# Recurrence with a block inverse, fused with an MLP: transposed input of the inverse laid out the other way round, one 16x16 merge moved from TensorE to VectorE, new instruction order

## The chip, the cores and the metric

The kernel runs on one core of a Trainium2 chip. The metric is the device time of one execution in microseconds (us); lower is better. A core has five engines that run side by side, each through its own instructions in a fixed order: TensorE (PE in the rows; PEld are its weight loads), VectorE (DVE), ScalarE (ACT), GpSimd (POOL) and SyncE (SP), which issues most of the transfers.

## What is computed

A recurrence over 768 steps for 4 x 8 heads with a 40 x 40 state each, and behind it a gated MLP on 3072 tokens. The reference, cut to its core:

```python
for t in range(S):                                   # S = 768, per batch and head
    y[:, :, t] = einsum('bhd,bhde->bhe', rt, state)
    Sa = einsum('bhde,bhe->bhd', state, at)
    state = state * wt - einsum('bhd,bhe->bhde', Sa, bt) + einsum('bhd,bhe->bhde', vt, kt)
x = y.transpose(0, 2, 1, 3).reshape(B * S, H * D)    # 3072 x 320
a, b = x @ w1, x @ w2                                # 320 x 1024 each
out = (a * b @ w3) @ w_out                           # 1024 x 1024, 1024 x 320
```

The weights come as 64-bit floats and are converted on the chip.

## The kernel before

The 768 steps are cut into 12 chunks of 64 (`NCH`, `C`). Inside a chunk the recurrence becomes matrix products and the inverse of a unit triangular 64 x 64 matrix for each head. The matrices of all heads lie in one tile: 128 partitions by 16 heads (`NPC`) by two halves of 32 columns, `JP`.

**Solve** (L648) inverts the 32 x 32 diagonal blocks, all on VectorE, as a sequence of small steps `so.x`. `f0` (tag `so.in`, L656) transposes the blocks from `JP` into the tile `TDX`. `dots` (L677) adds two steps to the sequence: a multiplication with broadcast operands into `tmp` (L680) and a sum over its last axis (L684). First the 8 x 8 triangles are inverted (seven pairs of steps with `A8` as an operand, results in `DG`), then pairs of 8 are merged to 16 x 16 (`Tp`, seen as `T32`), then pairs of 16 to 32 x 32. `A()` is the transposed input seen as row s, column t; `P8` is a piece of `TDX` that the inverse does not need, used for intermediate products. `f6` (`so.td`, L730) and `f7` (`so.tt`, L733) transpose the result back into the two halves of `TDX`.

The last merge, 16 to 32, runs in one of two ways. For chunks c >= `MERGED` it is eleven more steps on VectorE: five pairs of `dots` and one addition (L725). For chunks below `MERGED` TensorE does it after `so.tt`: 64 small products `so.m1` (L754), a copy to `Q16` on ScalarE (`so.q`), the products `so.m2`, a copy back into `TDX` (`so.t`), and a second `so.tt`.

**Join** (L766) joins the two 32 x 32 inverses of a head with the block below them: two products on TensorE (`jo.mm1`, `jo.mm2`, L782) with copies on ScalarE. `jo.mm1` needs `so.tt`; the copies `jo.tt` fill the tile `TT`, which the recurrence reads. `TDX` exists once, `JP` and `TT` twice.

**The rest.** `rec` (L870, tags `r.*`) runs the chunk's recurrence on TensorE, with ScalarE copies and VectorE masks (`r.u`, L921). `gather` moves the result into token order by transfers, `mlp` splits it into a high and a low part (`m.xh` at L971, `m.xl` at L974) and runs the MLP on TensorE: `m.mm1` (L987, eight matmuls of 256 columns a group) and `m.mm2` (L1012). `m.gl` (L1003) makes the low part of the gated product, on VectorE or GpSimd. At the start `convert` and `weights` turn the weights into matmul form (`cv.*`, `w.hi`, `w.lo` at L527), and `product` (L539) multiplies `w3` by `w_out` beforehand. The first MLP needs all of `w.lo`. The `ck.*` steps read the weights once more late in the run and check that the fast conversion was allowed; they use the tiles `JP` and `TDX` when the solves leave them free.

**Order.** Every operation is recorded first. A table of numbers written out by hand, `RANK`, gives each operation its place in the whole sequence (`place`, L300), and each engine runs its own operations in that order. A second table, `ON`, says for some kinds on which engine each instance runs (`d` VectorE, `p` GpSimd, `a` ScalarE). An instruction of GpSimd with two inputs waits for the last such instruction of VectorE placed before it ("port" in `place`).

Of the kernel before, what the change touches and what calls it, by code (L numbers as in the profile page):

```python
# [33 lines left out]
MERGED = 2  # L34
# [21 lines left out]
    "cv.sign": "aaddddaaadaaaaaaaaadaaaddaddadd",  # L56
    "cv.add": "ddddpdddddddddddddddpdpddddppdd",
    "w.lo": "dddddddddddd",
    "sc.aa": "dddddpdppddppddppdpppdpd",
    "sc.xs": "ddpdddpdddddpdpdddpdpddd",  # L60
    "m.gl": "dddpdpdpppppdpddpppppppppppppppdpppdpppdpppppddp",
    "ck.sq": "ddaaadaddaadaddddadaddddddddddd",
}
RANK = {kind: [int(n) for n in ranks.split()] for kind, ranks in {
# [1198 lines left out]
```

## Time and profile before

| | before |
|---|---|
| median of 3 runs | 624.01 us (620.47 to 626.31) |
| profiled execution: time / span | 625.69 us / 624.0 us |
| TensorE busy | 554.2 us, 89% of the span |
| VectorE busy | 514.1 us, 82% |
| ScalarE busy | 408.6 us, 65% |
| GpSimd busy | 160.4 us, 26% |
| mean granted TensorE clock | 0.971 of full speed |

The profile comes from one execution. Busy times are unions over the span; TensorE's matmuls overlap, so their mean durations are longer than the time each adds. A wait names the instruction that waits and what ended the wait. The clock is a share of full speed (2.4 GHz); the lower level is 0.5 (1.2 GHz).

### The profile page before, as it was taken

The page shows a single profiled execution, that of the slowest core. Times are in us where ns is not written, and L with a number is a line of the kernel's source. Part 1 is how long each engine was busy: PE and PEld are TensorE (multiplying, and loading weights), DVE is VectorE, ACT ScalarE, POOL GpSimd, SP SyncE. Part 2 cuts the span into 40 slices and gives each one's busy share as a digit, 9 for nine tenths or more (in the row PEclk, how much of TensorE's full clock was granted, in tenths as well). Part 3 has the DMA queues.
Part 4 walks back from the last instruction along what each step waited for, and adds up shares of the span by engine and source line. Part 5 has one row for each costly group of instructions (what it writes and reads, how often), then busy time and mean ns, then how long its engine had stood idle before and what let it go on. Part 6 is the DMA issues. An engine that isn't in the chain of part 4 may idle for free.

```text
span 624.0 us, 27212 instructions
## 1 busy us (share of the span) xinstructions
PE 554.2 (89%) x11970; PEld 498.7 (80%) x11970; DVE 514.1 (82%) x946; ACT 408.6 (65%) x883; POOL 160.4 (26%) x224
## 2 busy tenths in 40 slices
PE   0477998899998999999998999998998999999993
PEld 0355776799888988898897888898887989989993
DVE  5897897899599698896798797896996998977773
ACT  7787867954746747638646568648377568477552
POOL 3014131202521413034133133144043132131100
PEclk9997996999899899999998999999998999999998
DMA  8999777232143155322442343712643535237671
GB/s 226 293 251 268 224 222 203 71 94 81 50 107 111 33 133 141 87 72 61 112 116 66 98 112 98 193 43 72 180 117 105 153 87 148 85 83 242 212 246 56
DMA packets 56813, 83.48 MB, mean 134 GB/s; under 512 B 30320, under 2 KB 38000, under 8 KB 56688
## 3 DMA queue, kind: packets, MB, share of 16 engines
q1 hardware_dynamic: 56300, 81.34, 46.9%
q8 instruction: 96, 1.57, 1.1%
q10 hardware_dynamic: 388, 0.33, 0.2%
q14 instruction: 29, 0.24, 0.1%
HBM read 72.99 MB, written 3.93 MB: 123 GB/s over the span
## 4 chain that ended last, share of the span: by engine, by line
DVE 39%; PE 35%; ACT 10%; DMA 7%; issue 6%; POOL 1%; SPq 0%; ACTq 0%; DVEq 0%; POOLq 0%
DVE tmp L680 12%; PE bank L987 12%; PE bank L870 10%; PE bank L539 5%; DVE TDX L684 3%; DMA raw<-in_w3t_dram 3%; PE bank L1012 3%; DVE Tp L684 3%; PE bank L628 3%; DVE ga L1000 2%; ACT JP L329 2%; ACT TT L329 2%; DVE TDX L656 2%; PE bank L782 2%; DVE fm L578 2%
## 5 line engine op out<-in xcount | busy, mean ns | idle before, releaser
L987 PE MATMUL bank<-xs,W 128*128 128x256 f32 x1536 | 211.9, 291 | 0.6 <-DVE xs L974 0.6
L987 PEld LDWEIGHTS bank<-xs,W 128*128 128x128 f32 x1536 | 192.6, 193 | 8.4 <-issue 1.2
L1003 POOL TENSOR_TENSOR gl<-ga,gh 128x512 fp32r<-128x512 f32 x35 | 45.0, 1286 | 175.2 <-DVE tmp L680 52.0
L830 POOL TENSOR_SCALAR_AFFINE_SELECT vg<-vg 64x256 f32<-64x256 f32 x96 | 42.3, 447 | 124.7 <-DVE tmp L680 41.9
L1012 PE MATMUL bank<-W3h,gh 128*128 128x320 f32 x192 | 62.7, 327 | 0.7 <-ACT gh L329 0.7
L1012 PE MATMUL bank<-W3h,gl 128*128 128x320 f32 x192 | 60.1, 313 | 2.8 <-DVE gi L596 1.7
L1012 PE MATMUL bank<-W3l,gh 128*128 128x320 f32 x192 | 59.5, 310 | 0.0
L680 DVE TENSOR_TENSOR tmp<-Tp,TDX 128x256 f32<-128x256 f32 (+2 forms) x54 | 57.8, 1071 | 1.0
L628 PE MATMUL bank<-aa,xx 40*64 40x64 f32 x1536 | 31.4, 235 | 29.9 <-DVE xx L600 19.3
L628 PEld LDWEIGHTS bank<-aa,xx 40*64 40x64 f32 x1536 | 28.3, 148 | 33.2 <-issue 21.0
L329 ACT ACTIVATE JP<-bank 32x256 f32<-32x256 f32 (+2 forms) x120 | 45.5, 379 | 11.9 <-PE bank L628 7.5
L329 ACT ACTIVATE ga<-bank 128x512 f32<-128x512 f32 x48 | 28.6, 596 | 32.8 <-PE bank L987 31.8
L870 PE MATMUL bank<-un,bk 64*64 64x104 f32 (+1 forms) x768 | 44.3, 252 | 4.7 <-DVE un L921 4.1
L870 PE MATMUL bank<-hs,TT 64*64 64x104 f32 x768 | 45.1, 255 | 2.9 <-ACT TT L329 1.4
L329 ACT ACTIVATE gh<-ga 128x512 fp32r<-128x512 f32 x48 | 30.3, 631 | 25.8 <-DVE ga L1000 24.7
L644 POOL TENSOR_SCALAR_AFFINE_SELECT lm<-lm 64x512 f32<-64x512 f32 x48 | 35.3, 740 | 45.4 <-DVE tmp L680 18.0
L870 PE MATMUL bank<-vg,bk 64*64 64x104 f32 (+1 forms) x768 | 44.2, 253 | 0.0
L1000 DVE TENSOR_TENSOR ga<-bank,ga 128x512 f32<-128x512 f32 x48 | 32.9, 685 | 13.5 <-PE bank L987 7.6
L921 DVE TENSOR_TENSOR un<-bank,mask_h 128x416 f32<-128x416 f32 x48 | 28.2, 587 | 18.9 <-PE bank L870 18.6
L870 PEld LDWEIGHTS bank<-un,bk 64*64 64x64 f32 (+1 forms) x768 | 35.4, 123 | 10.0 <-DVE un L921 7.1
L539 PE MATMUL bank<-wof,w3f 128*128 128x320 f32 x128 | 42.4, 487 | 0.0
L870 PEld LDWEIGHTS bank<-hs,TT 64*64 64x64 f32 x768 | 35.2, 133 | 6.4 <-ACT TT L329 2.4
(126 smaller groups left out, 1263.7 us busy)
## 6 DMA issues: line engine op xcount, KB each, us to landing
rv<-in_rv_dram SPq DMA_DIRECT2D x24, 588.0 KB
xx<-in_fmx_dram SPq DMA_DIRECT2D x24, 448.0 KB
raw<-in_w3t_dram SPq DMA_DIRECT2D x16, 512.0 KB
JP<-in_w3t_dram SPq DMA_DIRECT2D x11, 512.0 KB
fm<-in_fmg_dram SPq DMA_DIRECT2D x24, 227.5 KB
aa<-in_fma_dram SPq DMA_DIRECT2D x24, 224.0 KB
raw<-in_w_dram SPq DMA_DIRECT2D x10, 512.0 KB
vg<-in_vt_dram SPq DMA_DIRECT2D x48, 80.0 KB
```

The costliest lines, as they stand in the source:

```text
L329: act.activation(out_, in_, AF.Copy, scale=scale)
L539: pe.matmul(out=pt.t[:, 0:DM], lhsT=w[:, j], rhs=wof[:, j], start=(j == 0), stop=(j == NJ - 1))
L628: pe.matmul(out=bank(s)[64 * z:64 * z + 64, i, p], lhsT=X[r, p, z], rhs=aa.t[r, i, p], start=True, stop=True)
L644: op("ca.mask", lambda q=q: pool.affine_select(out=lm.t[q], in_=lm.t[q], pattern=[[0, 2 * NP], [1, C]], compare_op=ALU.is_gt, fill=0.0, ba ...
L680: dve.tensor_tensor(out=scratch(*shape), in0=x().to_broadcast([128, *shape]), in1=y().to_broadcast([128, *shape]), op=ALU.mult)
L684: dve.tensor_reduce(out=out_(), in_=scratch(*shape), axis=mybir.AxisListType.X, op=ALU.add)
L830: op("pa.mask", lambda q=q, vg=vg: pool.affine_select(out=vg.t[q, :, 0:C], in_=vg.t[q, :, 0:C], pattern=[[0, NP], [1, C]], compare_op=ALU. ...
L870: pe.matmul(out=out_(ab ^ z, p), lhsT=left(ab, ab ^ x, p), rhs=right(ab ^ x, p), start=start and p == 0, stop=True, skip_group_check=True)
L987: pe.matmul(out=pt.t[:, TOK * x:TOK * x + TOK], lhsT=WT[k][:, cs], rhs=xs.t[:, z], start=(n == 0), stop=(n == 7))
L1000: op("m.ab", lambda a=a, pt=pt: dve.tensor_tensor(out=a.t, in0=wide(pt), in1=a.t, op=ALU.mult), r=[pt], w=[a])
L1003: both("m.gl", lambda e, a=a, j=j: e.tensor_tensor(out=gl.t[:, j:j + 2], in0=a.t, in1=gh.t[:, j:j + 2], op=ALU.subtract), r=[a, (gh, j)], ...
L1012: pe.matmul(out=pt.t[:, 0:DM], lhsT=l.t[:, j, ts], rhs=W3[r][:, j], start=(j == 0 and n == 0), stop=(j == NJ - 1 and n == 2))
```

## The change

Three edits in one.

1. `f0` writes the transposed input with t innermost in `TDX`: element (s, t) lies at 32 s + t, before at 32 t + s. The views `A`, `A8` and `P8` follow: `A` now has stride 1 along t, 32 along s; `P8` moves to the last 256 words, rows 24 to 31 of the new layout. The output of the transposing instruction is no longer contiguous.
2. `MERGED` goes from 2 to 1: chunk 1's last merge runs on VectorE, as in the chunks behind it. Chunk 0 keeps TensorE.
3. `RANK` and `ON` are new throughout.

```diff
-MERGED = 2
+MERGED = 1
 ON = {
-    "w.lo": "dddddddddddd",
+    "w.lo": "ddppdpdddddp",
-    "m.gl": "dddpdpdpppppdpddpppppppppppppppdpppdpppdpppppddp",
+    "m.gl": "dddpdpddpppppppppdpppppdddpppppddppdpppdpddddddp",
 RANK = ...
         def f0():
             src = jp.t[:, :, 0].rearrange("q p t -> q t p").unsqueeze(2).to_broadcast([128, 32, 2, 16])
-            dve.transpose(out=tdx.t.rearrange("q (t r p) -> q t r p", r=2, p=16), in_=src)
+            dve.transpose(out=tdx.t.rearrange("q (r p t) -> q t r p", r=2, p=16), in_=src)
 
         def A():
-            return tdx.t.rearrange("q (t s) -> q s t", s=32)
+            return tdx.t.rearrange("q (s t) -> q s t", t=32)
 
         def A8(s):
-            v = tdx.t[:, 33 * s + 32:33 * s + 33]
-            return bass.AP(v.tensor, v.offset, (v.ap[0], (264, 4), (32, 7 - s)))
+            v = tdx.t[:, 33 * s + 1:33 * s + 2]
+            return bass.AP(v.tensor, v.offset, (v.ap[0], (264, 4), (1, 7 - s)))
 
         def P8():
-            return tdx.t[:, 0:256].rearrange("p (q s) -> p q s", s=32)[:, :, 8:24]
+            return tdx.t[:, 768:1024].rearrange("p (q s) -> p q s", s=32)[:, :, 0:16]
```

Counted over the whole table `ON`: `m.gl` runs on VectorE 13 times before and 20 after (35 and 28 on GpSimd); `w.lo` 12 and 8 (0 and 4 on GpSimd); `sc.xs`, the scaling of `xx`, 18 and 17 (6 and 7); `cv.sign` 12 and 11 (19 and 20 on ScalarE); `ck.sq` 22 and 15 (9 and 16 on ScalarE).

TensorE in chunk 1, around the join, before. `rv,SB` are the recurrence's products with the state, `TDX,Q` is `so.m2`, `wof,w3f` the weight product, `TDX,JP` at L782 the join, `un,aa` the next step of the recurrence:

```order
L870 MATMUL bank_156<-rv_122,SB 40x104 x2
L870 MATMUL bank_154<-rv_122,SB 40x104 x2
L754 MATMUL bank_153<-TDX_121,Q_83 32x16 x64
L539 MATMUL bank_155<-wof,w3f_178 128x320 x4
L782 MATMUL bank_157<-TDX_121,JP_145 32x32 x32
L539 MATMUL bank_155<-wof,w3f_178 128x320 x4
L782 MATMUL bank_153<-TDX_121,JP_145 32x32 x32
L870 MATMUL bank_158<-un_129,aa_114 64x104 x2
```

The same place after:

```order
L870 MATMUL bank_152<-un_129,aa_114 64x104 x2
L870 MATMUL bank_155<-un_130,aa_114 64x104 x2
L539 MATMUL bank_154<-wof,w3f_177 128x320 x4
L782 MATMUL bank_157<-TDX_121,JP_145 32x32 x32
L539 MATMUL bank_154<-wof,w3f_177 128x320 x4
L782 MATMUL bank_153<-TDX_121,JP_145 32x32 x32
L628 MATMUL bank_158<-aa_113,xx_109 64x64 x2
```

The products `so.m1` and `so.m2` of chunk 1 are gone, and the recurrence step with `un,aa` stands ahead of the join instead of behind it.

VectorE at the end of chunk 1's solve, before: from the first `so.tt` (L733) to the second, with steps of the weight conversion (L453, L460, L446, L544) and of the next chunk's scaling between them:

```order
L733 STREAM_TRANSPOSE TDX_121<-TDX_121 128x512
L578 SCALAR_TENSOR_TENSOR fm_106<-fm_106,first 104x520
L453 TENSOR_SCALAR rs_167<-raw_165 128x512
L544 TENSOR_TENSOR W3l<-bank_154,W3h 128x320
L592 TENSOR_TENSOR gt_120<-fm_106,gi_119 104x512
L596 SCALAR_TENSOR_TENSOR gi_119<-gt_120,gi_119 104x512
L460 ISA w3f_178<-w3f_178,rs_169 128x1024
L600 TENSOR_TENSOR xx_109<-xx_109,gi_119 104x1024
L460 ISA mf_172<-mf_172,rs_167 128x1024
L446 TENSOR_SCALAR mf_171<-raw_164 128x512
L578 SCALAR_TENSOR_TENSOR fm_105<-fm_105,first 104x520
L733 STREAM_TRANSPOSE TDX_121<-TDX_121 128x512
```

The end of the same solve after:

```order
L684 TENSOR_REDUCE Tp<-tmp 128x8x8
L930 TENSOR_TENSOR y_142<-bank_154,fm_105 104x4x64
L680 TENSOR_TENSOR tmp<-Tp,TDX_121 128x512
L684 TENSOR_REDUCE R_151<-tmp 128x8x8
L725 TENSOR_TENSOR TDX_121<-R_151,TDX_121 128x8x8
L578 SCALAR_TENSOR_TENSOR fm_106<-fm_106,first 104x520
L680 TENSOR_TENSOR tmp<-TDX_121,DG 128x512
L684 TENSOR_REDUCE Tp<-tmp 128x8x8
L730 STREAM_TRANSPOSE TDX_121<-Tp 128x32x16
L592 TENSOR_TENSOR gt_120<-fm_106,gi_119 104x512
L544 TENSOR_TENSOR W3l<-bank_153,W3h 128x320
L733 STREAM_TRANSPOSE TDX_121<-TDX_121 128x512
```

The steps of the merge stand where the wait for the second `so.tt` was filled with other work; there is one `so.tt`.

TensorE at chunk 2's join, before. `xs,W` are matmuls of the first MLPs:

```order
L987 MATMUL bank_156<-xs_1769,W_1_1481 128x256 x2
L987 MATMUL bank_156<-xs_1769,W_3_1482 128x256
L987 MATMUL bank_156<-xs_1769,W_4_1483 128x256 x2
L782 MATMUL bank_152<-TDX_121,JP_144 32x32 x32
L987 MATMUL bank_153<-xs_1769,W_0_102 128x256 x2
```

After:

```order
L987 MATMUL bank_156<-xs_1611,W_1_1327 128x256 x2
L987 MATMUL bank_156<-xs_1611,W_3_1328 128x256
L987 MATMUL bank_156<-xs_1611,W_4_1329 128x256 x2
L782 MATMUL bank_152<-TDX_121,JP_144 32x32 x32
L987 MATMUL bank_155<-xs_1611,W_0_102 128x256 x2
```

The join has not moved against the MLP groups around it.

## Rows read from the trace of the kernel before

**Rows 1.** Busy us (and instructions) of each engine by stage; stage, length first.

```profile
0.00:124.00 124.00, 87.13 (x2116) 67.17 (x2120) 101.04 (x197) 97.17 (x198) 30.98 (x56) 0.93 0.80 220
124.00:560.00 436.00, 412.68 (x9200) 380.04 (x9189) 374.18 (x667) 276.14 (x626) 121.71 (x162) 0.98 0.38 101
```

The columns are PE, PEld, DVE, ACT, POOL, then PE's clock, the DMA share and GB/s.

**Rows 2.** TensorE's waits from 124 to 560: us in total, times, longest.

```profile
PE bank L782 <- DVE TDX L733: 5.9, 6, 1.7
PE bank L870 <- DVE un L921: 3.7, 8, 0.7
...
PE bank L987 <- DVE xs L974: 0.6, 1, 0.6
```

**Rows 3.** The chain that ended last, by engine and line; L680's busy time.

```profile
DVE 39%; PE 35%; ACT 10%; DMA 7%; issue 6%; POOL 1%; SPq 0%; ACTq 0%; DVEq 0%; POOLq 0%
DVE tmp L680 12%; PE bank L987 12%; PE bank L870 10%; PE bank L539 5%; DVE TDX L684 3%; DMA raw<-in_w3t_dram 3%; PE bank L1012 3%; DVE Tp L684 3%; PE bank L628 3%; DVE ga L1000 2%; ACT JP L329 2%; ACT TT L329 2%; DVE TDX L656 2%; PE bank L782 2%; DVE fm L578 2%
...
0.00:560.00 560.00, 109.45 (x182) 0.97 0.47 128
```

**Rows 4.** VectorE by shape in solve: count | busy us, mean ns | idle before.

```profile
L680 DVE TENSOR_TENSOR tmp<-Tp,TDX 128x512 f32<-128x512 f32 x20 | 22.4, 1118 | 0.5
...
L680 DVE TENSOR_TENSOR tmp<-Tp,TDX 128x1024 f32<-128x1024 f32 x10 | 20.5, 2054 | 0.1
...
L680 DVE TENSOR_TENSOR tmp<-Tp,TDX 128x256 f32<-128x256 f32 x24 | 14.9, 623 | 0.4
...
L680 DVE TENSOR_TENSOR tmp<-TDX,DG 128x512 f32<-128x512 f32 x20 | 14.4, 720 | 0.5
L684 DVE TENSOR_REDUCE Tp<-tmp 128x64 f32<-128x512 f32 x20 | 13.7, 686 | 0.5
...
L684 DVE TENSOR_REDUCE TDX<-tmp 128x64 f32<-128x1024 f32 x10 | 12.2, 1217 | 0.2
...
L680 DVE TENSOR_TENSOR tmp<-TDX,DG 128x256 f32<-128x256 f32 x24 | 10.3, 431 | 0.3
...
L725 DVE TENSOR_TENSOR TDX<-R,TDX 128x64 f32<-128x64 f32 x10 | 2.2, 225 | 0.3
```

**Rows 5.** The same view: the transposes, and two multiplications on strided operands.

```profile
L656 DVE STREAM_TRANSPOSE TDX<-JP 128x1024 f32<-128x1024 f32 x12 | 24.1, 2011 | 4.1 <-ACT JP L329 2.7 <-PE bank L782 1.3
...
L730 DVE STREAM_TRANSPOSE TDX<-Tp 128x512 f32<-128x512 f32 x12 | 13.3, 1105 | 0.4
...
L733 DVE STREAM_TRANSPOSE TDX<-TDX 128x512 f32<-128x512 f32 x14 | 9.9, 709 | 2.8 <-ACT TDX L329 2.4
...
L696 DVE TENSOR_TENSOR tmp<-DG 128x128 f32<-128x128 f32 x12 | 4.8, 402 | 0.3
L703 DVE TENSOR_TENSOR Tp<-tmp,DG 128x128 f32<-128x128 f32 x12 | 4.7, 393 | 0.3
```

**Rows 6.** The merge on TensorE, two chunks; a piece of the chain (start, us).

```profile
L754 PE MATMUL bank<-TDX,Q 32*32 32x16 f32 x256 | 3.9, 206 | 3.9 <-issue 2.1 <-ACT Q L329 1.7
...
L754 PE MATMUL bank<-TDX,JP 32*32 32x16 f32 x256 | 2.5, 180 | 0.0
...
123.39 0.94 ACT xs L971 x2
```

**Rows 7.** Two stretches behind waits for the solve, columns as in rows 1.

```profile
156.00:164.00 8.00, 6.87 (x160) 6.68 (x161) 3.76 (x5) 5.54 (x12) 4.96 (x5) 0.79 0.36 93
336.00:344.00 8.00, 6.43 (x157) 5.95 (x156) 4.64 (x6) 6.56 (x15) 5.64 (x9) 0.79 0.27 83
```

**Rows 8.** Groups of instructions: the low part of the gated product, and `w.lo`.

```profile
L1003 POOL TENSOR_TENSOR gl<-ga,gh 128x512 fp32r<-128x512 f32 x35 | 45.0, 1286 | 175.2 <-DVE tmp L680 52.0 <-ACT gh L329 37.5 <-ACT gi L582 25.9
...
L1003 DVE TENSOR_TENSOR gl<-ga,gh 128x512 fp32r<-128x512 f32 x13 | 9.2, 711 | 1.3 <-ACT gh L329 1.3
...
L527 DVE TENSOR_TENSOR W<-mf,W 128x512 fp32r<-128x512 f32 (+1 forms) x12 | 8.5, 719 | 3.7 <-ACT W L329 3.7
```

More of the change, by code (lines that the diff above doesn't have):

```diff
@@ L55 @@
 ON = {
-    "cv.sign": "aaddddaaadaaaaaaaaadaaaddaddadd",
-    "cv.add": "ddddpdddddddddddddddpdpddddppdd",
-    "w.lo": "dddddddddddd",
-    "sc.aa": "dddddpdppddppddppdpppdpd",
-    "sc.xs": "ddpdddpdddddpdpdddpdpddd",
-    "m.gl": "dddpdpdpppppdpddpppppppppppppppdpppdpppdpppppddp",
-    "ck.sq": "ddaaadaddaadaddddadaddddddddddd",
+    "cv.sign": "dddadaaaddddaaaadaaaaaaddaaaaaa",
+    "cv.add": "dddddddddddddddddddppdpdpdpdddd",
+    "w.lo": "ddppdpdddddp",
+    "sc.aa": "ddddddddpdpppppppdppddpd",
+    "sc.xs": "ddddddpppdddddpdddpdpdpd",
+    "m.gl": "dddpdpddpppppppppdpppppdddpppppddppdpppdpddddddp",
+    "ck.sq": "dddaaddadaaaaadddadaaaddaadadda",
 }
 RANK = {kind: [int(n) for n in ranks.split()] for kind, ranks in {
[184 rows of a table removed]
[184 rows of a table added]
 }.items()}
```

366 rows, old and new, of the table RANK are left out of this document.

## The prediction

> **What bounds the kernel now.** I read first how busy the engines are by stage. Up to 124 us (weight conversion and the first two chunks) DVE works 101.04 of 124 us and TensorE 87.13; from 124 to 560 us TensorE works 412.68 of 436 us and DVE 374.18 [rows 1]. So in the long middle stage TensorE has only 436 − 412.68 = 23.3 us of idle time and DVE 61.8 us: work taken off DVE cannot shorten the stage by itself, it can only close TensorE's gaps.
>
> Then I read what ends TensorE's waits in that stage. The largest entry is L782 (the first product of `join`) waiting for L733 (the last transpose of `solve`): 5.9 us in 6 waits, the longest 1.7 [rows 2]. Four of the ten solves are finished before TensorE asks for them, six are late. The next is L870 waiting for L921 (`r.u`), 3.7 us in 8 short waits. Last I read the chain that ended last: DVE holds 39% and TensorE 35% of the span, and L680, the multiplications inside `solve`, alone 12% [rows 3]. The chain hops from DVE (solve) to TensorE (join, recurrence, MLP) and back, once in a chunk. The reader should see a kernel that two in-order engines limit in turns, with TensorE the tighter.
>
> **The solve's reads.** In `solve` the multiplications of `dots` read the transposed input `A()` with the last axis t innermost. Before, neighbours in t lie 32 words apart; after, they are adjacent. The price of a 32-word hop stands in the trace: with `A()` as an operand 512 elements take 1118 ns and 1024 take 2054, that is (2054 − 1118)/512 = 1.83 ns per element; the same instruction on contiguous operands (`tmp<-TDX,DG`) takes 431 for 256 and 720 for 512, 1.13 ns per element [rows 4]. So I price the new forms by the contiguous rows: 256 elements 623 → 431, 512 elements 1118 → 720, and 1024 elements 2054 → 720 + 2 × (720 − 431) = 1298. A solve that merges on DVE has two of 256, two of 512 and one of 1024 (24, 20 and 10 in the run): 2 × 0.192 + 2 × 0.398 + 0.756 = 1.94 us less. The seven small multiplications with `A8` keep a second operand (`DG`, 8 words apart in its inner axis); L696, which reads two strided operands, takes 402 ns for 128 elements and L703 with one takes 393 [rows 5]. One strided operand costs nearly all that two cost, so I give these seven no gain.
>
> The Trainium skill says the same of such reads (Vector Engine (DVE) Microarchitecture Reference, section 5.2, Measured stream behaviour on trn2): a port runs at full rate only on runs of at least two adjacent words, 1.054 ns per column against 1.73 with one source hopping; by its figures the 1024 form would save 0.69 us, by the rows 0.76.
>
> **The transposing input (L656)** is where the hop goes to. It reads `JP` 64 words apart already, and from now on it also writes 32 words apart. Now it takes 2011 ns for 1024 elements. No row has both. Bounds: nothing, if the read hides the write; or the whole price of a strided write, L730 (strided write, 1105 ns for 512) less L733 (contiguous, 709), 0.396 for 512, so 0.79 us here [rows 5]. The nearest pair, L696 against L703, gives 9 ns on 128, 0.07 on 1024; I take 0.1 us a solve, 1.2 over twelve, and keep 0.79 (9.5 over twelve) for the range. The transpose loses 0.1, so a full solve is 1.84 us shorter.
>
> **Chunk 1's merge.** The two products and two copies go (`so.m1`, `so.m2`, `so.q`, `so.t`), with one L733 of 0.71. L754 has 3.9 + 2.5 us in two chunks, so TensorE loses 3.2 us of work [rows 6]. DVE gains eleven instructions: multiplications 0.72, 1.30, 0.72, 0.72, 0.72, four reductions of 512 at 0.69 and one of 1024 at 1.22, one addition of 64 elements at 0.23 [rows 4]: 4.18 + 2.76 + 1.22 + 0.23 = 8.4 us. Net on DVE in chunk 1: 8.4 − 0.7 − 2 × 0.19 + 0.1 = +7.4. This lies before 124 us, where the first MLP waits for its last weights: the chain there ends in ACT's `xs` at 123.39 [rows 6], TensorE waits 0.6 us for it [rows 2]. I cost both parts at nothing: TensorE's 3.2 us is hidden by that wait, DVE's 7.4 by its 23 us of idle time before 124 us and by four `w.lo` that go from DVE to POOL (4 × 0.72 = 2.9 [rows 8]). On TensorE the join of chunk 1 now waits for a solve that is longer on DVE but needs no second trip over TensorE and ACT; queued behind it are the rest of the `W3` product and chunk 1's recurrence, which the first MLP does not need. Without that cover the first MLP starts 7.4 − 2.9 = 4.5 us later.
>
> **The order.** The places are alike: in chunk 2 the join's first product still stands between the same MLP matmul groups. No transfer is added or taken away; SP's issues change places by a few, which I cost at nothing (a late first load would show in the last rival's stretch). Of the choices of engine one bears on the middle stage: `m.gl` goes from POOL to DVE seven times net, 7 × 0.711 = 5.0 us more on DVE and 7 × 1.286 = 9.0 less on POOL [rows 8]. On DVE they stand in front of solve steps; I charge the chain's DVE share, 39%, so 2.0 us. Seven `ck.sq` go from DVE to ACT; these check pieces lie late in the run, ACT works 276.14 of the 436 us of the middle stage [rows 1], and I cost them at nothing; uncovered they would be 7 × 0.72 = 5 us on ACT (by the 512-column row of L527 [rows 8]).
>
> **The sum.** Six waits for the solve, none longer than 1.7 us, against solves shorter by 1.84: −5.9. The clock: after the two longest of them TensorE's granted clock is 0.79 on average over 8 us, a part of it at the lower level of 1.2 GHz instead of 2.4, after TensorE stood idle [rows 7]; where the engine is busy that is 2 × 8 × 0.21 = 3.4 us lost, given back when the waits go. Against that +2.0 for `m.gl`. Together −5.9 − 3.4 + 2.0 = −7.3 us. The profiled execution took 625.69 us (span 624.0), so 618.4 by its own time; it is 1.7 above the median of the runs shown, 624.01, and by that the forecast is 616.7. What is late next is `r.u`, the copies of `TT` and the last check pieces at the end; none of these does the change touch.
>
> **Rivals.**
> *DVE is the real bound.* For: it holds 39% of the chain, and L680's 12% of 624 is 75 us out of its 109.45 [rows 3]. Then 68% of what the multiplications lose in ten solves, 0.68 × 19.4 = 13.2, comes off, the dips with it: −13.2 − 3.4 + 2.0 = −14.6, 609. Against: TensorE's 23 us of gaps would have to shrink by more than half.
> *TensorE is the bound and the gaps only move.* Its waits for `r.u` and the other short ones grow as the solve's shrink, the idle and the clock dips stay; with half of the 5.9 won and the 2.0 paid, 623.
> *The transpose pays in full.* With 0.79 for the write a solve is 1.15 us shorter, so the waits of 1.7 and the next below it stay in part (about 1.0 us of the 5.9) and so do the dips: −4.9 + 2.0, 621. For: L730 shows that a strided write costs as much as a strided read. The skill's same section has a destination stepping 24 words at 2.50 ns per column, against 1.73 for a hopping source; by that the transposes would lose 12 × 0.79 = 9.5 us, the same as this bound. L730's 1105 for 512, about 1.9 per element with its fixed part, does not show the 2.50.
> *Slower: chunk 1's merge holds up the first MLP.* If DVE's idle time before 124 us lies where the merge cannot use it (it waits there for ACT and for weight data), the first MLP starts 4.5 us late or, if the `w.lo` on POOL finish late too, the whole 7.4 us late. TensorE has nothing else to do then, and everything behind shifts. It decides from 7.3 us on, when it eats all of the later gain; with the gaps staying as well it is 624 + 7.4 = 631.
>
> **How the numbers follow.** The forecast, 616.7 with an own range of 612 to 621, has 0.45; DVE as the bound 0.17; the gaps that move 0.17; the transpose in full 0.11; the late MLP 0.10. A measurement of this kernel can tell about 1% from no change, so faster means below 617.8 and slower above 630.2. Faster: seven tenths of the forecast's case and all of the first rival, 0.48; slower: nearly all of the last, 0.09; the rest 0.43. The range runs from 607 to 626: it leaves out the late MLP and the low end of the first rival.
>
> **What would show it.** In the profile after, the multiplications with `A()` at about 0.43, 0.72 and 1.30 us for 256, 512 and 1024 elements; L656 near 2.1 (2.8 would be the rival); the seven `A8` products unchanged. TensorE's wait for L733 should fall from 5.9 us to under 1.5, its idle time between the first MLP and 560 us from 23 to about 17, and the clock should stay at the upper level after chunk 2's join. The first `xs` should still start near 123 us; at 128 or later the last rival holds. I am wrong if the solve waits go and another entry of the same size stands in their place, or if the stage before the first MLP has become longer.

## The result and the profile after

The changed kernel takes 605.72 us (median of 4 runs, 601.54 to 607.49) against 625.16 us for the kernel before beside it; the ratio is 0.968, with a 95% interval of 0.959 to 0.977. The profiled execution took 607.17 us, its span 605.5. Measured again beside the layout alone, the ratio was 0.972 (0.967 to 0.976). The gain is 2.9 to 3.2%, 17 to 20 us, where 616.7 us, 1.2%, was forecast; the time lies just below the range of 607 to 626.

First the multiplications of the solve. VectorE by shape in the changed kernel (count | busy us, mean ns | idle before):

```profile
L656 DVE STREAM_TRANSPOSE TDX<-JP 128x1024 f32<-128x1024 f32 x12 | 26.7, 2226 | 6.8 <-ACT JP L329 3.8 <-ACT TT L329 3.0
...
L680 DVE TENSOR_TENSOR tmp<-Tp,TDX 128x512 f32<-128x512 f32 x22 | 15.2, 693 | 0.4
L680 DVE TENSOR_TENSOR tmp<-TDX,DG 128x512 f32<-128x512 f32 x22 | 15.2, 692 | 0.4
...
L680 DVE TENSOR_TENSOR tmp<-Tp,TDX 128x1024 f32<-128x1024 f32 x11 | 13.6, 1239 | 0.2
...
L680 DVE TENSOR_TENSOR tmp<-Tp,TDX 128x256 f32<-128x256 f32 x24 | 11.1, 461 | 0.4
...
L680 DVE TENSOR_TENSOR tmp<-DG,TDX 128x196 f32<-128x196 f32 x12 | 6.2, 516 | 0.3
```

With `A()` as an operand 512 elements now cost what the contiguous instruction costs (693 and 692 ns), 1024 take 1239 and 256 take 461; the prices were right within 0.06 us [rows 4]. The largest `A8` product barely moves, from 527 to 516 ns; the seven together take 0.17 us less in a solve. The transpose L656 takes 2226 ns, not 2011 [rows 5]: 0.22 us more for writing 32 words apart as well.

Then the stages, cut at the first and the eleventh `m.xl` (L974), which stands on VectorE at the start of an MLP. Before, then after (stage, length, then busy PE, PEld, DVE, ACT, POOL; PE's clock, DMA share, GB/s):

```profile
0.00:124.30 124.30, 87.43 (x2132) 67.47 (x2133) 101.04 (x197) 97.47 (x200) 30.98 (x56) 0.93 0.80 220
124.30:556.70 432.40, 409.08 (x9071) 376.83 (x9062) 373.22 (x666) 272.64 (x619) 119.90 (x160) 0.98 0.37 101
556.70:624.00 67.30, 57.70 (x779) 54.43 (x777) 39.86 (x83) 38.51 (x67) 9.50 (x9) 0.96 0.61 187
```

```profile
0.00:119.20 119.20, 85.48 (x1824) 64.12 (x1828) 105.10 (x204) 96.49 (x197) 28.59 (x56) 0.94 0.76 223
119.20:535.60 416.40, 401.23 (x9057) 370.54 (x9052) 351.69 (x667) 274.99 (x619) 122.52 (x159) 0.99 0.39 106
535.60:605.50 69.90, 60.06 (x866) 56.24 (x854) 37.50 (x83) 42.72 (x74) 5.22 (x8) 0.94 0.59 181
```

The first stage is 5.1 us shorter, the middle one 16.0, the last one 2.6 longer. In the middle TensorE's idle time falls from 23.3 to 15.2 us and its busy time by 7.9 us, although it runs nearly the same number of matmuls there (9071 and 9057 in the profile); the granted clock is 0.99 of full speed, not 0.98. The first stage scatters: two executions of one and the same kernel, the layout alone below, have their first `m.xl` at 122.1 and at 125.0 us, so the 5.1 us there need not all be the change's.

TensorE's waits in the middle stage after (us in total, times, longest):

```profile
PE bank L870 <- DVE un L921: 6.4, 8, 1.5
PE bank L870 <- issue: 3.9, 5, 2.1
...
PE bank L628 <- POOL aa L589: 0.4, 1, 0.4
PE bank L782 <- DVE TDX L733: 0.2, 1, 0.2
```

The 5.9 us of waiting for the solve [rows 2] are 0.2. `r.u` (L921) holds TensorE for 6.4 us where it was 3.7.

And the chain that ended last, which before was DVE 39% and PE 35% [rows 3]:

```profile
PE 47%; DVE 17%; ACT 16%; DMA 8%; issue 5%; SPq 4%; POOL 1%; ACTq 0%; DVEq 0%; POOLq 0%
```

These shares are coarse: in two executions of the layout alone DVE has 17% and 25%.

### The profile page after: what moved, and what is told of

Same layout as the page of the kernel before. It is cut to its first block, busy times and chain, and to the rows that moved or that the text cites. A ratio compares the mean times of both kernels' runs of the same rounds, so it can differ in the third digit from the quotient of the medians.

```text
span 605.5 us, 26713 instructions
## 1 busy us (share of the span) xinstructions
PE 546.8 (90%) x11714; PEld 490.9 (81%) x11714; DVE 494.3 (82%) x950; ACT 414.2 (68%) x889; POOL 156.3 (26%) x222
## 4 chain that ended last, share of the span: by engine, by line
PE 47%; DVE 17%; ACT 16%; DMA 8%; issue 5%; SPq 4%; POOL 1%; ACTq 0%; DVEq 0%; POOLq 0%
PE bank L987 19%; PE bank L870 12%; PE bank L1012 5%; ACT JP L329 4%; ACT TT L329 4%; PE bank L539 3%; SPq L946 3%; DVE tmp L680 3%; PE bank L628 2%; PE bank L845 2%; DMA raw<-in_wo_dram 2%; DMA raw<-in_w3t_dram 2%; PE bank L821 1%; DVE TDX L656 1%; DVE un L921 1%
## 5 line engine op out<-in xcount | busy, mean ns | idle before, releaser
L987 PE MATMUL bank<-xs,W 128*128 128x256 f32 x1536 | 209.0, 288 | 0.0
L987 PEld LDWEIGHTS bank<-xs,W 128*128 128x128 f32 x1536 | 190.1, 191 | 7.3 <-issue 0.8
L830 POOL TENSOR_SCALAR_AFFINE_SELECT vg<-vg 64x256 f32<-64x256 f32 x96 | 40.3, 426 | 145.9 <-DVE tmp L680 72.2
L1003 POOL TENSOR_TENSOR gl<-ga,gh 128x512 fp32r<-128x512 f32 x28 | 36.1, 1290 | 121.7 <-DVE tmp L680 46.1
L870 PE MATMUL bank<-un,bk 64*40 64x104 f32 (+1 forms) x768 | 44.8, 255 | 10.0 <-DVE un L921 7.8
L644 POOL TENSOR_SCALAR_AFFINE_SELECT lm<-lm 64x512 f32<-64x512 f32 x48 | 33.5, 699 | 76.2 <-DVE tmp L680 25.4
L329 ACT ACTIVATE JP<-bank 64x256 f32<-64x256 f32 (+2 forms) x120 | 45.2, 378 | 10.8 <-PE bank L628 8.3
L870 PE MATMUL bank<-hs,TT 64*64 64x104 f32 x768 | 46.6, 260 | 2.2 <-ACT TT L329 1.7
L870 PEld LDWEIGHTS bank<-un,bk 64*40 64x40 f32 (+1 forms) x768 | 35.7, 124 | 13.6 <-DVE un L921 11.2
L921 DVE TENSOR_TENSOR un<-bank,mask_h 128x416 f32<-128x416 f32 x48 | 28.1, 584 | 22.7 <-PE bank L870 22.6
L870 PE MATMUL bank<-vg,bk 64*40 64x104 f32 (+1 forms) x768 | 45.0, 255 | 0.3 <-issue 0.2
L870 PEld LDWEIGHTS bank<-hs,TT 64*64 64x64 f32 x768 | 36.7, 136 | 7.5 <-ACT TT L329 3.0
L680 DVE TENSOR_TENSOR tmp<-Tp,TDX 128x256 f32<-128x256 f32 (+2 forms) x57 | 39.9, 700 | 1.0
```

Of the source, the lines that this page charges most:

```text
L329: act.activation(out_, in_, AF.Copy, scale=scale)
L644: op("ca.mask", lambda q=q: pool.affine_select(out=lm.t[q], in_=lm.t[q], pattern=[[0, 2 * NP], [1, C]], compare_op=ALU.is_gt, fill=0.0, ba ...
L680: dve.tensor_tensor(out=scratch(*shape), in0=x().to_broadcast([128, *shape]), in1=y().to_broadcast([128, *shape]), op=ALU.mult)
L830: op("pa.mask", lambda q=q, vg=vg: pool.affine_select(out=vg.t[q, :, 0:C], in_=vg.t[q, :, 0:C], pattern=[[0, NP], [1, C]], compare_op=ALU. ...
L870: pe.matmul(out=out_(ab ^ z, p), lhsT=left(ab, ab ^ x, p), rhs=right(ab ^ x, p), start=start and p == 0, stop=True, skip_group_check=True)
L921: dve.tensor_tensor(out=un[i].t, in0=view(hp[i]), in1=mask_h.unsqueeze(1).to_broadcast([128, NP, N]), op=ALU.mult)
```

## The experiments

Each ratio is against the kernel before in the same session. The first four split the change.

**The layout alone.** The four edits of `f0`, `A`, `A8` and `P8`; everything else is as before:

```diff
-            dve.transpose(out=tdx.t.rearrange("q (t r p) -> q t r p", r=2, p=16), in_=src)
+            dve.transpose(out=tdx.t.rearrange("q (r p t) -> q t r p", r=2, p=16), in_=src)
...
```

> Only the layout of the transposed input is new; MERGED stays 2, order and engine choices are those of before. Both theories: a full solve is 1.94 us shorter on its multiplications and 0.2 longer on the transposing input, VectorE loses about 17 us of work. Theory SOLVE (the gain is the shorter solve on the chain between the two engines): most of the 18.5 us between the two profiled spans appears with the old order, 13 us or more, ratio below 0.980. Theory ORDER (the new order makes the gain, the solve's waits alone are worth my 7 us or less): ratio 0.988 to 0.998.

Measured: 606.82 us, 0.975 (0.971 to 0.979). The layout brings 15 us with the order of before, where my sum had 9.3 for it (5.9 for waits and 3.4 for the clock), and it brings most of what the whole change brings.

**The new order without the layout**: the changed kernel with the four edits undone.

> The changed kernel with the old layout: new order, MERGED = 1, but reads 32 words apart. VectorE gets about 19 us of work back (eleven full solves at 1.94 less 0.2 for the transpose). Theory SOLVE: the new order was made for short solves and cannot hide long ones; 620 us or more, ratio 0.99 to 1.01. Theory ORDER: 608 to 614, ratio 0.975 to 0.985.

Measured: 619.01 us, 0.994 (0.991 to 0.997). New order and `MERGED = 1` are worth 3.7 us by themselves. The ratio is the one that the theory of the solve gave, though the time lies a little below its 620: the order is no loss with long solves, and it is a small part.

**MERGED = 1 alone**, old layout and old order:

```diff
-MERGED = 2
+MERGED = 1
...
```

In the table `RANK` the eleven merge steps of chunk 1 get evenly spaced places between its two old `so.tt`, with `so.td` behind them, and one `so.tt` is left out.

> Only MERGED = 1: the eleven merge steps of chunk 1 are put evenly between the places of its two old output transposes, everything else stands as before. My prediction gave it nothing (0 to +7.4 us if the first MLP is held up). Theory that the round trip over TensorE and ACT in chunk 1 cost the early stage time: 2 to 5 us faster, ratio 0.992 to 0.997. Theory that VectorE's 8.4 us of added work hold up the first MLP: 4 to 7 us slower, ratio 1.007 to 1.012.

Measured: 626.8 us, 1.0065 (1.0033 to 1.0097): 4 us slower. In its profile the first `m.xl` stands at 127.2 us, 26.1 us after the last piece of weights is asked for (101.1); before, it is 19.7 us after it (104.7), and in the two executions of the layout alone 20.7 and 20.6. The merge on VectorE does hold up the first MLP when the order is not made for it. It costs 4 us, where 7.4 was the price without any cover (in this run all `w.lo` stay on VectorE).

**Layout and MERGED = 1 under the old order.**

> Layout and MERGED = 1 together under the old order and engine choices. Theory SOLVE: close to the changed kernel, ratio 0.970 to 0.980. Theory ORDER: like e1, ratio 0.985 to 0.998; the distance to the changed kernel's 0.968 is then the order's own share.

Measured: 609.53 us, 0.980 (0.974 to 0.986); its first `m.xl` too stands late, at 127.0, 25.0 us after the last weights are asked for. By the middles of the intervals, which overlap, the steps add up: the layout gives 15, `MERGED = 1` costs 3 to 4, the new order gives that back and a little more.

Two runs ask which solves count, the seven others keeping the old layout.

```diff
+NEW = (2, 5, 6, 7, 10)          # the second run: (3, 4, 8, 9, 11)
-            return tdx.t.rearrange("q (t s) -> q s t", s=32)
+            return tdx.t.rearrange("q (s t) -> q s t" if c in NEW else "q (t s) -> q s t", s=32)
...
```

**The five solves that TensorE visibly waits for.**

> Before, with the new layout only in chunks 2, 5, 6, 7 and 10, the five solves that TensorE visibly waits for at the join (5.5 us of the 5.9). The other seven solves keep the old layout. Theory WAITS (my prediction: only the solves that are late at the join matter): all of the layout's gain, 12 to 15 us, ratio 0.975 to 0.982. Theory CHAIN (VectorE runs through the middle stage without slack that matters, every solve's 1.7 us come off in full): half of the gain, 6 to 9 us, ratio 0.986 to 0.991.

**Five solves that are ready when TensorE asks.**

> Before, with the new layout only in chunks 3, 4, 8, 9 and 11, the solves that are ready when TensorE asks. Theory WAITS: no gain, 0 to 2 us, ratio 0.997 to 1.0. Theory CHAIN: as much as in the five others, 6 to 9 us, ratio 0.986 to 0.991.

Measured: 612.54 us, 0.980 (0.978 to 0.982), and 615.69 us, 0.986 (0.983 to 0.989). The first came out as the theory of the waits had it, the second as the theory of the chain. The five late solves bring 12.6 us; but the five others bring 8.6 us where the theory of my prediction gave them at most 2. That is 1.7 us each, just what one of them is shorter by (1.94 less 0.22). And they do so without touching the wait on which I had built the sum; TensorE's waits for the solve in the second kernel's middle stage:

```profile
PE bank L787 <- DVE TDX L738: 5.5, 5, 1.7
```

What shrank there are TensorE's waits for other work. Before, these stood behind those of [rows 2] in size:

```profile
PE bank L870 <- POOL vg L830: 2.5, 4, 1.0
PE bank L628 <- DVE aa L589: 1.8, 1, 1.8
PE bank L1012 <- DVE gi L596: 1.7, 1, 1.7
```

With the five other solves shorter, the `vg` entry is 0.9, `aa` 1.5, and the wait at the MLP's second product 1.1 us. Two of these waits cost the clock as well. The middle stage before has four stretches partly at the lower level: the two of [rows 7] behind waits for the solve, and two behind the waits for `aa` and `gi`:

```profile
200.00:208.00 8.00, 6.56 (x96) 6.41 (x96) 6.25 (x9) 5.20 (x11) 4.17 (x8) 0.79 0.02 7
470.00:478.00 8.00, 5.65 (x131) 5.05 (x134) 3.69 (x5) 5.06 (x14) 1.23 (x4) 0.79 0.52 155
```

With the five other solves shorter these two are gone, and the two behind the solve are still there:

```profile
154.00:162.00 8.00, 6.49 (x156) 6.30 (x157) 4.13 (x5) 5.16 (x12) 5.35 (x5) 0.79 0.36 98
331.00:339.00 8.00, 6.76 (x206) 6.33 (x210) 4.20 (x6) 6.77 (x16) 4.71 (x8) 0.79 0.19 68
```

With the five late ones shorter, one is left, behind the wait for `aa`. That only the waits for the solve count fell here. The two gains together, 21 us, are more than the 15 of all solves, so they overlap; no run shows why.

**The new order with chunk 1's merge on TensorE.** The changed kernel with `MERGED = 2`; the four merge operations and the second transpose stand where chunk 1's steps stood, as far as free PSUM banks allowed.

> The changed kernel with chunk 1's last merge back on TensorE: the eleven steps leave VectorE, the four operations of the merge and the second transpose stand in chunk 1 where the steps stood. MERGED = 1 alone cost 4 us under the old order. Theory that VectorE's 8.4 us before the first MLP are a loss in any order: 2 to 5 us faster than the changed kernel, 600 to 604, ratio 0.960 to 0.966. Theory that the new order is made for it and the early stage gains from the missing round trip: 2 to 5 us slower than the changed kernel, ratio 0.972 to 0.980.

Measured: 614.19 us, 0.982 (0.979 to 0.984), 6 to 8 us slower than the changed kernel by the ratios of the two sessions. Its first `m.xl` stands at 131.9 us. But the last weights are asked for at 109.6 us there, not at 99.5 as in the changed kernel, ten of the 13 us by which that `m.xl` is later. So this may be my placing of the operations; that the merge on VectorE is the better one in the new order is not shown.

**The old order up to place 584, the new one behind it**, with new layout and `MERGED = 1`.

> New layout and MERGED = 1; the order and engine choices of before up to place 584 (the first MLP and the last solve step of chunk 1 are before it), the new order behind it. The old order in full took 0.980, the new one 0.968. If the order's gain lies in the early stage (the first MLP started 5 us earlier in the changed kernel): 0.977 to 0.983. If it lies in the middle stage: 0.966 to 0.972.

Measured: 613.1 us, 0.979 (0.975 to 0.983), as the old order throughout (0.980). So the later part of the new order shows no gain by itself; what the new order brings lies in the first stage, or is spoiled at the seam.

Four runs of one session compare the best versions.

**The changed kernel again, and the layout alone again.**

> The changed kernel itself, measured beside the layout alone, to see what MERGED = 1 and the new order add together to the layout (0.9754 in e1). If they add nothing: 0.973 to 0.978, no difference to e10. If they add what the single intervals suggest: 0.966 to 0.971.

> The layout alone under the old order, again, beside the changed kernel: 0.973 to 0.978 by e1. Its distance to e9 is the share of MERGED = 1 and the order.

Measured: 603.78 us, 0.972 (0.967 to 0.976), and 604.57 us, 0.975 (0.970 to 0.979). The two cannot be told apart. Their profiles differ by stage: the first `m.xl` at 118.7 us in the changed kernel and 125.0 under the old order (122.1 in its other execution), the last stage 69.8 against 67.1 us.

**The new order up to place 798, the old one behind it**, with new layout and `MERGED = 1`.

> New layout and MERGED = 1; the new order and engine choices up to place 798 (into chunk 3, behind the first two MLPs' start), the order of before behind it. If the new order's gain is the early stage (first MLP at 119 us, not 127) and its later part costs 2 to 5 us against the old one: 600 to 604, ratio 0.960 to 0.966, faster than the changed kernel. If the parts belong together: 0.970 to 0.980.

Measured: 601.36 us, 0.970 (0.966 to 0.974). The lowest median of all, but its interval overlaps widely with the changed kernel's. Its first `m.xl` stands at 122.2 us.

**The engine choices of `m.gl` as before**, in the changed kernel:

```diff
-    "m.gl": "dddpdpddpppppppppdpppppdddpppppddppdpppdpddddddp",
+    "m.gl": "dddpdpdpppppdpddpppppppppppppppdpppdpppdpppppddp",
```

> The changed kernel with the engine choices of m.gl as before (13 on VectorE, not 20). My sum charged the seven on VectorE 2.0 us. If that holds: 2 us faster than the changed kernel, 0.964 to 0.967. If the new order was made for them and TensorE waits for GpSimd's slower ones: 2 to 6 us slower, 0.972 to 0.979.

Measured: 606.01 us, 0.975 (0.971 to 0.979). It is not faster than the changed kernel: the 2.0 us that I charged for these seven do not show. Whether they are a gain stays open.

The last three ask what limits the middle stage, on top of the layout alone.

**One more multiplication inside each solve** (from chunk 2 on), and **the same one behind it**:

```diff
+        def extra():
+            dve.tensor_tensor(out=tmp, in0=tmp, in1=tmp, op=ALU.mult)
         def f6():
+            if c >= 2:                  # second run: at the end of f7, behind the last transpose
+                extra()
```

> The layout alone (0.975 in e1 and e10), with one useless contiguous multiplication of 1024 elements (about 1.1 us) into the scratch tile before the output transposes of each solve from chunk 2 on: ten of them, 11 us more on VectorE and every solve 1.1 us longer. If every microsecond of a solve still counts: 9 to 12 us slower than the layout alone, ratio 0.990 to 0.994. If TensorE has become the bound with the new layout, which the chain (TensorE 58%, VectorE 17%) says: 1 to 4 us, ratio 0.977 to 0.982.

> The same useless multiplication put behind the last transpose of each of these solves, so that VectorE has the same added work but no solve is longer. If VectorE's total work sets the middle stage: like e13. If the solve's own length does: 0 to 3 us slower than the layout alone, ratio 0.975 to 0.980, clearly under e13.

Measured: inside 619.26 us, 0.996 (0.992 to 1.001); behind 610.67 us, 0.980 (0.974 to 0.985). The useless instruction was longer than I had reckoned, as the two kernels' rows by shape show:

```profile
L729 DVE TENSOR_TENSOR tmp<-tmp 128x1024 f32<-128x1024 f32 x10 | 16.9, 1694 | 0.3
```

```profile
L729 DVE TENSOR_TENSOR tmp<-tmp 128x1024 f32<-128x1024 f32 x10 | 14.9, 1486 | 0.0
```

So 16.9 us inside the solves cost about 13 us (0.021 of 623, plus or minus 3, against the layout alone in its two sessions), and 14.9 us behind them about 3 (0.0045 of 623, plus or minus 4). The same engine and nearly the same work: the place decides. With the extra work inside, the price stands in the wait table too. TensorE's wait for the solve in the layout alone, then with it:

```profile
PE bank L782 <- DVE TDX L733: 0.6, 2, 0.4
```

```profile
PE bank L787 <- DVE TDX L738: 13.1, 9, 2.8
```

**More work on TensorE**: the first product of the join twice, from chunk 2 on.

```diff
-        op("jo.mm1", lambda: product(p1.t, 0, half(1)), ...)
+        op("jo.mm1", lambda: [product(p1.t, 0, half(1)) for _ in range(2 if c >= 2 else 1)], ...)
```

> The layout alone, with the first product of the join done twice from chunk 2 on (the same values written again): ten times 0.74 us, 7.4 us more on TensorE and the join as much later. If TensorE is now the bound: 6 to 9 us slower than the layout alone, ratio 0.985 to 0.990. If VectorE still is: 0 to 3 us, ratio 0.975 to 0.980.

Measured: 616.57 us, 0.989 (0.984 to 0.995), about 9 us, plus or minus 4, for 7.4 us of work by my estimate. TensorE's work at the join counts for most of its price or all of it as well.

What lies behind this shows when the middle stage is cut where a solve begins (`so.in`) and ends (`so.tt`). The ten solves from chunk 2 on, and the nine stretches between them, as sums over the stretches (length, busy us; the means are for one stretch). Before:

```profile
sum 302.58, PE 286.74 PEld 264.62 DVE 291.04 ACT 161.66 POOL 81.83; mean PE 28.67 PEld 26.46 DVE 29.10 ACT 16.17 POOL 8.18
sum 125.01, PE 117.89 PEld 108.03 DVE 78.30 ACT 106.36 POOL 37.18; mean PE 13.10 PEld 12.00 DVE 8.70 ACT 11.82 POOL 4.13
```

The layout alone:

```profile
sum 286.65, PE 279.72 PEld 260.68 DVE 272.61 ACT 160.30 POOL 82.00; mean PE 27.97 PEld 26.07 DVE 27.26 ACT 16.03 POOL 8.20
sum 123.13, PE 115.30 PEld 105.34 DVE 77.32 ACT 107.88 POOL 36.23; mean PE 12.81 PEld 11.70 DVE 8.59 ACT 11.99 POOL 4.03
```

With the extra multiplication inside, then behind the solve; then with the join's product twice:

```profile
sum 301.89, PE 283.39 PEld 263.31 DVE 287.97 ACT 161.85 POOL 94.00; mean PE 28.34 PEld 26.33 DVE 28.80 ACT 16.19 POOL 9.40
sum 119.02, PE 113.32 PEld 104.73 DVE 76.59 ACT 105.98 POOL 31.72; mean PE 12.59 PEld 11.64 DVE 8.51 ACT 11.78 POOL 3.52
```

```profile
sum 287.12, PE 279.93 PEld 261.74 DVE 272.17 ACT 159.68 POOL 80.89; mean PE 27.99 PEld 26.17 DVE 27.22 ACT 15.97 POOL 8.09
sum 126.58, PE 116.78 PEld 105.82 DVE 90.56 ACT 108.41 POOL 40.45; mean PE 12.97 PEld 11.76 DVE 10.06 ACT 12.05 POOL 4.49
```

```profile
sum 283.74, PE 278.85 PEld 260.94 DVE 272.32 ACT 159.81 POOL 82.44; mean PE 27.88 PEld 26.09 DVE 27.23 ACT 15.98 POOL 8.24
sum 131.74, PE 122.86 PEld 112.23 DVE 77.53 ACT 108.57 POOL 35.95; mean PE 13.65 PEld 12.47 DVE 8.61 ACT 12.06 POOL 3.99
```

Inside the solves VectorE works 291.0 of 302.6 us, 96%; between them 78.3 of 125.0, 63%. Of its idle time 11.5 us lie inside and 46.7 between, four fifths. The layout takes 16 us off the first kind of stretch and 2 off the second. The useless work inside puts 15.2 us back and takes 4.1 off the second kind, 11 us together; the same work behind the solves raises VectorE's busy time between them by 13.2 us and the stretch by 3.5. The join lies between two solves, and there TensorE's double product adds 8.6 us, of which the stretches inside give 2.9 back.

## Why the prediction was wrong

The prices of the instructions were right; the step from a shorter solve to a shorter run was not. Point by point:

- **The solve's reads**: right. 1.94 us a solve were priced; by the rows after it is 2 × 0.16 + 2 × 0.43 + 0.82 = 2.0 us.
- **The transposing input**: taken at 0.1 us, measured 0.22, far from the 0.79 of the rival. The Trainium skill's table (Vector Engine (DVE) Microarchitecture Reference, section 5.2) has 1.98 ns per column with all three streams of a two-source instruction hopping against 1.73 with one; as an estimate for this instruction, which has one source, 0.25 × 1024 gives 0.26 us, and the trace's 0.22 is near it. Its 2.50 for a destination that steps 24 words is not shown here at 32.
- **The sum** is the step that failed: "Six waits for the solve, none longer than 1.7 us, against solves shorter by 1.84: −5.9", all that it has for TensorE's idle time. I read VectorE's 61.8 us of idle time [rows 1] as slack that lies everywhere, and let only those solves count whose end TensorE is seen to wait for. But about 47 us of it lies between the solves. Inside a solve VectorE has 4% left, so time taken off there moves the end of the solve, and with it the in-order work behind it on both engines, whether or not a wait stands at that join. The run on the five other solves shows it: 8.6 us, the full price, with the waits for the solve at 5.5 us.
- **What the 16.0 us of the middle stage are**, where −7.3 was forecast. The waits for the solve went, −5.7, as forecast. TensorE's other idle time fell by 2.4 us, for which the sum had nothing. The clock gave 3.4. The other 4.5 us are TensorE's busy time beyond what the clock explains, and the prediction has no term for them. The layout alone splits its 17.6 us of profiled middle stage (432.4 to 414.8, first to eleventh `m.xl`; 15 in the whole time) in the same way: 8.5 of idle time, 5.0 of clock, about 4 of other busy time.
- **The clock** came out right in size, by luck. The two stretches that were counted are gone, 3.4 us; but four had run partly at the lower level (0.79 over 8 us each, 6.7 us). In the changed kernel there is a new one twice as long, at a gap of 2.1 us on L870 for which the profile names no releaser, 3.4 us again; in the layout alone one of the old length is left:

```profile
208.00:224.00 16.00, 13.56 (x283) 11.93 (x274) 12.03 (x28) 5.90 (x15) 2.92 (x5) 0.79 0.53 145
```

```profile
453.00:461.00 8.00, 5.37 (x119) 4.84 (x123) 2.73 (x4) 4.20 (x12) 1.20 (x3) 0.79 0.51 155
```

- **The other busy time** goes with the layout and not with the length of the solve. With the useless work inside, TensorE's busy time in the middle stage stays at 401.4 us, with two stretches partly at the lower level, against 409.1 before with four. Three kernels have none there: the new order with the old layout, then the old order up to place 584 and the new order up to place 798, both with the new layout:

```profile
120.50:547.20 426.70, 402.11 (x9075) 369.69 (x9070) 368.84 (x665) 274.35 (x619) 121.42 (x159) 1.00 0.38 104
```

```profile
123.80:539.70 415.90, 399.09 (x9001) 368.24 (x8997) 351.50 (x666) 274.18 (x618) 122.15 (x157) 1.00 0.39 105
```

```profile
122.20:531.90 409.70, 398.82 (x9119) 369.51 (x9111) 352.89 (x667) 273.30 (x619) 120.30 (x162) 1.00 0.39 108
```

The profile's ends of matmuls are modelled, and no run asked what these 3 to 4 us are; their cause stays open.
- **`m.gl`**: +2.0 us were charged, and undoing the choice gained nothing that shows.
- **Chunk 1's merge**: taken at nothing. Under the old order it costs 3 to 4 us, by the rival's mechanism; my cover, VectorE's idle time before 124 us, hid only a part of the 7.4. From the request for the last piece of weights to the first `m.xl` it is 26.1 and 25.0 us there, against 19.7 before. In the changed kernel, with the merge, it is 19.7 again: the new order supplies the cover. VectorE then works 105.1 of 119.2 us before the first MLP instead of 101.0 of 124.3. That request comes 5.2 us earlier, but in kernels whose early order is that of before it lies anywhere from 100.1 to 104.7 us, so most of the 5.1 us of the first stage may be scatter. The two transfers on SyncE's queue, after and before:

```profile
99.49 0.52 SPq L443 DMA_DIRECT2D raw<-in_w_dram  x1
```

```profile
104.70 1.62 SPq L443 DMA_DIRECT2D raw<-in_w_dram  x1
```

- **The signs**: the wait for L733 fell to 0.2 us and TensorE's idle time to 15 us, as named. The sign of being wrong, another entry of the size of the solve's waits, came in part: `r.u` grew from 3.7 to 6.4 us, by less than half of what went.
- **The rivals**: "DVE is the real bound", 609 us with 0.17, was the nearest. Its reason was the better reading of the chain in [rows 3]; against it I had held TensorE's 23 us of gaps, which "would have to shrink by more than half". They shrank by a third (23.3 to 14.8 with the layout alone, 15.2 in the changed kernel), and the rest of the gain came from the clock and from TensorE's busy time.
- **The order**: I took it as neutral in the middle stage, and with the new layout it is (416.4 and 414.5 us in the changed kernel, 414.8 and 413.5 in the layout alone). What it brings by itself is the cover for `MERGED = 1`; together they add between nothing and 1% to the layout, which the session that has both could not separate.

Open: what the 3 to 4 us of TensorE's busy time are, whether `m.gl` and the new later order help at all, and how much of the slower merge on TensorE under the new order came from its placing.

## What to carry to other kernels

An engine's idle share over a stage says little; cut the stage where its long dependent sequence begins and ends, and read the share inside. If the engine is full there, a microsecond on or off the sequence counts for most of its length (16.9 us put in cost about 13 here), also where nobody is seen to wait for its end, and the same microsecond beside it counts little (14.9 us cost about 3). A wait table names where the loss comes to light, not how much would go if its cause got shorter. Look for every stretch in which TensorE's granted clock is below full speed, not only behind the wait that the change is to remove: here two of four stood behind others.

## What the runs showed of the hardware

The transposing instruction with 64-word steps in reading and 32-word steps in writing took 2226 ns for 1024 elements, 0.22 us more than with the read alone; L730, which only writes apart, costs 0.40 more than L733 on half the elements. Where both sides are strided, most of the write's price is hidden here: 0.22 of 0.79 us is seen. TensorE's busy time over nearly the same matmuls was 3 to 4 us lower with the new layout at the same granted clock (402.1 against 399.1 and 398.8); why is open. The useless multiplication with the same tile as both inputs and output took 1.49 and 1.69 us for 1024 elements, where the multiplication of two other tiles into it takes 1.24; why was not tried.
